# Attention times a gated token mixer on one core: where the last two heads' second span is divided, and where two output blocks are computed

## Chip, core and metric

The kernel runs on one core of a Trainium2 chip (trn2). The metric is device time in microseconds (us); the kernel before was timed at 1625.78 us, the median of three runs. The core's engines are named as the profile names them: PE (TensorE matmuls; PEld is its weight load), DVE (VectorE), ACT (ScalarE), POOL (GpSimd) and SP (SyncE, which here issues nearly all DMAs). SBUF is the on-chip memory that all of them reach, PSUM the accumulator that PE writes; PSUM has eight banks in this kernel, four called `sc`, three `mx`, one `av`.

## What is computed

```python
x  = A_x                                   # (1, 2048, 512), fp32
xn = layernorm(x)
# attention: 32 heads of 16
q, k, v = split(xn @ wqkv)                 # per head
o = softmax(q @ k.T / 4) @ v               # per head, 2048 x 2048 scores
s = concat(o) @ wo
# token mixer: an MLP along the token axis, 2048 -> 1792 -> 2048
h = layernorm(xn)
g = silu((gelu(h.T @ w1 + b1) @ w2 + b2).T)
out = x + s * g
```

## The kernel before

Everything is fp32 outside. A matmul that needs the accuracy is made of three products of a value's upper part (`[:, 0]`, fp32r) and its lower part (`[:, 1]`, the rest after subtraction): upper x upper, upper x lower, lower x upper.

**The main loop.** Heads are handled in 16 pairs, queries in two spans of 1024, keys in blocks of 128. The loop over `s` (L1274 on) takes two key blocks a turn; a turn is called a pair in this text. In every pair PE makes eight score matmuls for the row maxima (`mx`, L532, reduced by DVE at L536), eight score matmuls 22 steps behind (`sc`, L999, exponentiated by ACT at L1004 into `prob`), two groups of values (`av`, L1015), and some products of a queue called `fill`, written D in the order strings. `ORDERS` and `BEGIN` say in which order these matmuls stand in a pair, for 0, 4, 5 or 6 D; `BEGIN` holds only an entry for a first pair with six. Matmuls of 48 to 64 rows run two at a time, on the upper and the lower half of PE's rows, so one D costs one such slot.

**The fill.** It holds first the token mixer (14 blocks of 48 products, then 16 blocks of 42), then the output. `count()` (L1167 on) spreads each mixer block over as many pairs as give 16/3 products a pair; the block whose number is `SLOW` gets more pairs. 48 products so take nine pairs (6, 6, 6 and six times 5), 42 take eight. When the mixer is done, `both_pairs` runs two pairs at a time around one output block of nine products.

**The output.** Token block b (128 tokens, 16 of them) is the sum over four groups of eight heads of `oc[g, b // 4]` (attention result, heads x 16 = 128 rows, upper and lower part, 512 tokens) by the rows of `wo` of that group. Blocks 0 to 13 (`PARTS` = 14) get groups 0 to 2 in the main loop, nine products each; `part` (L919) evicts the sum with ACT (L922), POOL multiplies by the gate `g_d[b]` and adds x (L925, L926), SP stores it as `y_d[b]`. Group 3 can't be finished there: its heads 30 and 31 are the last pair.

**The ending** is `s` from `NU` = 512 on: no maxima are left, only scores, values and D, at three D a pair (`a_half`, the first of two halves) and from `s` = 524 six. In it come the group 3 products of blocks 8 to 13 and then 0 to 7, three each (42 in all). `finish` (L975) multiplies the sum with the gate and adds it to `y_d`, both on DVE, and writes out blocks 0 to 7. For blocks 8 to 15, which are the second span, rows 96 to 127 of `oc[3, 2]` and `oc[3, 3]` (heads 30 and 31) are zero (`made`, L790).

**After the last pair** (L1368 on) the second span of heads 30 and 31 is in PSUM as `av`: numerators and denominators of both heads and both halves of the span, 32 rows each. ACT copies it (`ev`). `one` turns it with four transposes so that tokens are rows, takes the reciprocal of the denominators, and spreads it over 32 columns a piece (L843, L845); `two` turns the spread reciprocals back (L854); `times` and `lower` multiply `ev` in its old layout and split it (L858, L859, L94). As that layout isn't the one of `wo`, `load_last_w` loads the rows of `wo` for the two heads once more into two zeroed tiles, and `split_last_w` splits them (L897). Each of blocks 8 to 15 then gets three products of these (`product`, L101 to L103). Blocks 14 and 15 get all four groups here as well, 24 products, `beside` (L1375), which are also used to keep PE busy during the division. `gated` (L1406) multiplies a block by its gate, `added` (L1410) adds what was summed before, on POOL or DVE, `in_parts` does both in two halves for the last block (L1417, L1418), and SP writes the blocks out (L1411, L1419).

Of the kernel before, what the change touches and what calls it, by code (L numbers as in the profile page):

```python
# [21 lines left out]
def tile_attention_token_mixer(ctx, tc, x, wqkv, wo, w1, b1, w2, b2, out):  # L22
# [746 lines left out]
    def divide(m, g, span):  # L769
# [17 lines left out]
        if last:  # L787
            for c in range(2):
                made.append(hu.tile([P, 2, 512], F32R, name="hu"))
                nc.gpsimd.memset(made[c][DH * n :, :, :].bitcast(F32), 0.0)  # L790
# [40 lines left out]
    def own(span, ev):  # L831
        rq = sm.tile([P, 4, 4], F32, name="rq", bufs=1)
        wide = el.tile([P, 512], F32, name="t", bufs=4)

        def one(pl=ps_mx, nm="mx", spread=1):

            ps = pl.tile([P, 512], F32, name=nm)
# [6 lines left out]
            for k in range(0, 4, 4 // spread):  # L844
                nc.vector.tensor_copy(  # L845
                    wide.rearrange("p (k j r) -> p k j r", k=4, j=4)[:, k : k + 4 // spread],
                    rq[:, k : k + 4 // spread].unsqueeze(3).to_broadcast([P, 4 // spread, 4, 32]),
                )

        def two(pl=ps_mx, nm="mx", ks=range(4)):  # L850

            ps = pl.tile([P, 512], F32, name=nm)
            for k in ks:
                nc.tensor.transpose(ps[:, k * P : (k + 1) * P], wide[:, k * P : (k + 1) * P], ident)  # L854
            return ps

        def times(ps, of, at):
            nc.vector.tensor_tensor(out=ev[:, at], in0=ps[:, at], in1=ev[:, at], op=OP.mult)  # L858
            nc.scalar.copy(of[:, 0, at], ev[:, at])  # L859

        def lower(of, at):
            sub(nc.vector, of[:, 1, at], ev[:, at], of[:, 0, at])

        if span == QH - 1:
            asides.extend((one, two, times, lower))
            return

        def move_in():
            ps = two()
            of = el.tile([P, 2, 512], F32R, name="uo")  # L870
            times(ps, of, slice(0, 512))
            lower(of, slice(0, 512))
# [7 lines left out]


    last_w = {}

    def load_last_w():
        for c in range(2):
            raw = last_w[c] = wp.tile([P, 4, P], F32, name="raw", bufs=3).rearrange("p a b -> p (a b)")
            nc.gpsimd.memset(raw, 0.0)
            for a in range(2):
                row = 32 * (2 * a + c) + DH * a
                h = H - 2 + a  # L890
                nc.gpsimd.dma_start(raw[row : row + DH, :], wo[DH * h : DH * (h + 1), :])

    def split_last_w():
        for c in range(2):
            raw = last_w[c]
            w = last_w[c] = el.tile([P, 2, 512], F32R, name="uo")
            nc.scalar.copy(w[:, 0, :], raw)  # L897
            after(2 + 2 * c, lambda w=w, raw=raw: sub(nc.vector, w[:, 1, :], raw, w[:, 0, :]))


# [6 lines left out]
    PARTS = NB // 2 + 6  # L907
    blocks = list(range(NB // 2, PARTS)) + list(range(NB // 2))

# [39 lines left out]
    def load_out(n):  # L949
        b = blocks[n]  # L950
        y, g = (("xt", "gt"), ("u", "sq"))[n % 2]
        if b < NB // 2:
            ys[b] = el.tile([P, D], F32, name=y)
            nc.sync.dma_start(ys[b], y_d[b])
        gts[b] = el.tile([P, D], F32, name=g)
        nc.sync.dma_start(gts[b], g_d[b])
# [3 lines left out]
    def plan_halves():  # L960

        rows = [oc[g, c][:, m, :].bitcast(F32) for c in range(NC - 1) for g in range(ND - 1) for m in range(2)]
        own = PARTS - NB // 2
        for n in range(own, len(blocks) - 3):
            b = blocks[n]
            in_halves.extend(((ys, b, y_d[b]), (gts, b, g_d[b])))
# [8 lines left out]
    def finish(n, ps):  # L975
        b = blocks[n]
        half = PARTS - NB // 2 <= n < len(blocks) - 3
        r = el.tile([P, D], F32, name="t", bufs=4) if half else gts[b]
        nc.vector.tensor_tensor(out=r, in0=ps, in1=gts[b], op=OP.mult)
        o = ys[b] if b >= NB // 2 else r  # L980
        nc.vector.tensor_tensor(out=o, in0=ys[b], in1=r, op=OP.add)
        if b < NB // 2:
            nc.sync.dma_start(out[b * P : (b + 1) * P, :], r)
        if n + 3 < PARTS - NB // 2:
            load_out(n + 3)
        elif n < PARTS - NB // 2:
            load_out(n + len(blocks) - PARTS + NB // 2)
# [35 lines left out]
    def rest():  # L1023
# [20 lines left out]
        for b in range(PARTS):  # L1044
# [6 lines left out]
        yield from until(lambda: now[0] >= NU and (ND - 1, QH - 1) in divided)  # L1051
        for n in range(3):
            load_out(n)
        plan_halves()
        for n, b in enumerate(blocks):
            if b == 0:
                yield from until(lambda: own_done and (ND - 1, 0) in divided)
# [3 lines left out]
            yield lambda n=n, ps=ps: finish(n, ps), back  # L1061
# [28 lines left out]
    SLOW = 4  # L1090
# [76 lines left out]
    def count():  # L1167
# [10 lines left out]
        return min(6, -(-left // -(-3 * left // (15 if i == SLOW else 16)))) if left > 0 else 0  # L1178
# [95 lines left out]
    for s in range(0, total + 1, 2):  # L1274
# [53 lines left out]
        else:  # L1328


            for i in range(2):

                a_half(*(heads[a][1][2 * i : 2 * i + 2] for a in range(2)), i == 0 or s >= NU + 2 * (PARTS - NB // 2))
# [8 lines left out]
            if s == NU + 4:  # L1342
                load_last_w()
            for _ in in_halves[:2]:
                load_half()
            if s == total - 6:
                split_last_w()
# [75 lines left out]
    for k in range(5):  # L1423
        if k < 4:
            times(shares[k], of, cols[k])
# [46 lines left out]
```

## Time and profile before

| | |
|---|---|
| three runs | 1625.33, 1625.78, 1626.55 us |
| profiled execution, span from first to last instruction | 1622.0 us |
| median less span (what lies around it) | 3.8 us |
| mean granted PE clock | 0.999 of full speed |
| PE, DVE, ACT, POOL busy | 1615.0, 1423.3, 1195.1, 561.6 us |
| last values matmul ends | 1604.4 us |
| last matmul ends | 1617.3 us |
| last output DMA is issued | 1619.0 us |

No separate time is given for the profiled execution; its span is the number against which a change is summed here. A busy share is an average over stages: the phase up to 150 us is projections, then comes the main loop to about 1550 us, the ending from there to 1604 us, and 18 us after the last values matmul. A busy PE is not PE at its peak, as its ends are modelled.

### The profile page before, as it was taken

The numbers are of one execution on the slowest core, as the hardware profiler recorded it, in microseconds if no ns is written. First come the engines' busy times: TensorE is split into PE (matmuls) and PEld (weight loads), VectorE is DVE, ScalarE is ACT, GpSimd is POOL, SyncE is SP. The second block draws the span as 40 slices with busy tenths as digits, with TensorE's granted clock in tenths as the row PEclk, the third lists the DMA queues.
The fourth block names the chain that finished last, engine by engine and source line by source line (L and its number), as shares of the span: only waits on it lengthen the run. The fifth ranks groups of instructions, "written<-read, shape, count | busy, mean of one in ns | idle before, by whom it ended". The sixth has DMA issues, their size and how long they took to land.

```text
span 1622.0 us, 31241 instructions
## 1 busy us (share of the span) xinstructions
PE 1615.0 (100%) x11937; PEld 877.2 (54%) x11937; DVE 1423.3 (88%) x2493; ACT 1195.1 (74%) x2311; POOL 561.6 (35%) x661
## 2 busy tenths in 40 slices
PE   9999999999999999999999999999999999999998
PEld 7888854544555544554554554545544544454544
DVE  7665999999999999999999999999999999999966
ACT  3333477777777777777877787777777778888885
POOL 1224844342244332342333332322222333642430
PEclk9999999999999999999999999999999999999999
DMA  7478441515133141826151522305151515444355
GB/s 237 181 242 204 114 92 41 95 41 75 41 70 73 30 82 34 241 70 108 41 86 38 82 65 40 77 22 76 38 85 37 112 39 84 123 101 130 106 192 192
DMA packets 152402, 155.60 MB, mean 96 GB/s; under 512 B 51564, under 2 KB 110188, under 8 KB 149180
## 3 DMA queue, kind: packets, MB, share of 16 engines
q1 hardware_dynamic: 147964, 152.87, 38.9%
q8 instruction: 94, 1.54, 0.4%
q0 software_dynamic: 4288, 0.73, 0.3%
q14 instruction: 56, 0.46, 0.1%
HBM read 101.86 MB, written 50.58 MB: 94 GB/s over the span
## 4 chain that ended last, share of the span: by engine, by line
PE 98%; DVE 1%; ACT 1%; DMA 0%; SPq 0%; issue 0%; POOL 0%; DVEq 0%
PE av L1015 31%; PE dn L1156 25%; PE sc L999 16%; PE mx L532 13%; PE sc L435 3%; PE dn L671 3%; PE mx L435 2%; PE av L435 1%; PE sc L101 0%; PE sc L103 0%; PE sc L102 0%; ACT prob L1004 0%; DVE mxp L536 0%; PE mx L999 0%; PE dn L1200 0%; PE mx L103 0%
## 5 line engine op out<-in xcount | busy, mean ns | idle before, releaser
L536 DVE TENSOR_REDUCE mxp<-mx 128x1 f32<-128x512 f32 x2026 | 1250.1, 680 | 116.1 <-PE mx L532 85.0
L1004 ACT ACTIVATE prob<-sc 128x512 f32<-128x512 f32 x2004 | 1040.4, 606 | 282.3 <-PE sc L999 117.6
L532 PE MATMUL mx<-big 48*128 48x512 f32 x2026 | 771.1, 418 | 0.1
L999 PE MATMUL sc<-big 50*128 50x512 f32 x2004 | 734.5, 411 | 0.0
L1015 PE MATMUL av<-prob,vp 128*32 128x512 f32 x4096 | 545.6, 604 | 0.3 <-DVE ev L722 0.2
L1156 PE MATMUL dn<-hu,wh 64*128 64x512 f32 x1520 | 508.0, 404 | 0.0
L999 PEld LDWEIGHTS sc<-big 50*128 50x128 f32 x2004 | 355.6, 186 | 230.0 <-ACT prob L1004 205.2
L532 PEld LDWEIGHTS mx<-big 48*128 48x128 f32 x2026 | 356.9, 185 | 187.7 <-DVE mxp L536 168.7
L1156 PEld LDWEIGHTS dn<-hu,wh 64*128 64x128 f32 x1520 | 271.8, 184 | 74.3 <-issue 49.5
L1156 PE MATMUL dn<-hu,wl 64*128 64x512 f32 x762 | 302.4, 397 | 0.0
L1015 PEld LDWEIGHTS av<-prob,vp 128*32 128x32 f32 x4096 | 80.9, 108 | 177.3 <-issue 165.0
L94 POOL TENSOR_TENSOR wl<-raw,wh 128x512 fp32r<-128x512 f32 x124 | 150.9, 1219 | 60.5 <-ACT wh L166 26.9
L1156 PEld LDWEIGHTS dn<-hu,wl 64*128 64x128 f32 x762 | 140.5, 184 | 12.6
L164 POOL CAST wh<-raw 128x512 fp32r<-128x512 f32 x104 | 60.6, 583 | 196.0 <-PE mx L532 76.0
L560 POOL CAST m<-f 16x128 fp32r<-16x128 f32 x31 | 8.7, 280 | 304.0 <-DVE f L548 303.9
L98 POOL DMA_DIRECT2D big<-m x124 | 65.8, 537 | 0.0
L1156 PE MATMUL dn<-wh,hu 64*128 64x512 f32 x168 | 59.7, 408 | 0.0
L621 POOL TENSOR_TENSOR sq<-u 128x512 f32<-128x512 f32 x11 | 11.5, 1041 | 133.8 <-ACT u L615 133.7
L708 POOL TENSOR_SCALAR t<-t 128x512 f32<-128x512 f32 x16 | 23.8, 1489 | 83.4 <-ACT t L705 83.4
L435 PE MATMUL sc<-xt,big 128*128 128x512 f32 x184 | 44.3, 389 | 0.0
L94 POOL TENSOR_TENSOR hu<-hx,hu 128x512 fp32r<-128x512 f32 x16 | 20.4, 1294 | 67.7 <-ACT hu L278 67.7
L671 PE MATMUL dn<-hu,wh 64*128 64x512 f32 x128 | 42.3, 392 | 0.0
(235 smaller groups left out, 1214.9 us busy)
## 6 DMA issues: line engine op xcount, KB each, us to landing
raw<-in_B_w_dram SPq DMA_DIRECT2D x104, 256.0 KB
big<-k_d SPq DMA_DIRECT2D x96, 128.0 KB
big<-q_d SPq DMA_DIRECT2D x96, 128.0 KB
q_d<-sg SPq DMA_DIRECT2D x16, 512.0 KB
k_d<-sg SPq DMA_DIRECT2D x16, 512.0 KB
num_d<-ev SPq DMA_DIRECT2D x30, 256.0 KB
u_d<-uo SPq DMA_DIRECT2D x14, 512.0 KB
hu<-u_d SPq DMA_DIRECT2D x14, 512.0 KB
```

The lines of the kernel that those rows point to most:

```text
L94: eng.tensor_tensor(out=o, in0=a, in1=b.bitcast(F32), op=OP.subtract)
L98: queue.dma_start(dst.bitcast(F32), src.bitcast(F32))
L164: nc.gpsimd.tensor_copy(whs[n][:, :m, :], raws[n][:, :m, :])
L435: nc.tensor.matmul(ps, w[part][:, kd, m], xt[kd][:, z, :], start=w is wh and z == 0 and kd == 0, stop=w is wl and kd == ND - 1,)
L532: nc.tensor.matmul(ps, q[o : o + 48, r * P : (r + 1) * P], k[o : o + 48, c * 512 : (c + 1) * 512], start=True, stop=True,)
L536: nc.vector.tensor_reduce(mxp[u // 16][:, a, r % 8, c : c + 1], ps, axis=AX.X, op=OP.max)
L671: nc.tensor.matmul(ps, w(slice(0, 64)), m(slice(0, 64)), start=first, stop=last)
L708: nc.gpsimd.tensor_scalar(t, t, 1.0, None, op0=OP.add)
L999: nc.tensor.matmul(ps, ks[p][o : o + 50, kb * P : (kb + 1) * P], qs[p][o : o + 50, at : at + 512], start=True, stop=True,)
L1004: nc.scalar.activation(e, ps, AF.Exp, scale=scale)
L1015: nc.tensor.matmul(av[32 * j : 32 * j + 32, :], vps[p][:, kb, 16 * a : 16 * a + 32], prob.pop((t, a, c)), start=kb == 0, stop=kb == NB - 1,)
L1156: made.append(lambda r=r, start=first and a == lead, stop=last and a != lead: nc.tensor.matmul(ps, w(r), m(r), start=start, stop=stop,))
```

## The change

The second span of heads 30 and 31 is now divided while tokens are rows. After the first four transposes and the two reciprocals, four DVE multiplications read the turned numerators in PSUM and write the quotients into a zeroed tile (`apart`, cleared by POOL at `s` = 528) at the columns that are rows 96 to 127 of the group. Eight transposes turn this back, two for each half of each of the two chunks; ACT copies rows 96 to 127 as the upper part straight into `oc[3, 2]` and `oc[3, 3]`, DVE subtracts for the lower part. So these operand tiles become complete, and blocks 8 to 15 get group 3 once, after the last pair, with the ordinary weights (24 products). The zeroing of rows 96 to 127, `load_last_w`, `split_last_w` and the group 3 products of blocks 8 to 13 in the ending are gone.

The places that these left in the ending are filled: `PARTS` is 15, of which the main loop does 13 and the ending's first pairs do blocks 13 and 14, group by group in turns, so that two PSUM banks are held at once. Only block 15 is summed after the last pair (nine products in place of 24). As the main loop has one output block less, `SLOW` names two more mixer blocks, 8 and 11, which take ten pairs (eight with 5, two with 4) in place of nine. The last additions are shared out anew: blocks 0 to 4 of the closing order on POOL, then the split block, then two on DVE.

```diff
-    PARTS = NB // 2 + 6
+    PARTS = NB - 1
+    LATE = NB - 3
+    HALVES = 5
...
-        for b in range(PARTS):
+        def whole_part(b):
             yield from until(lambda: all((g, b // (NB // QH)) in divided for g in range(ND - 1)))
...
+        for b in range(LATE):
+            yield from whole_part(b)
+        yield from until(lambda: now[0] >= NU)
         plan_halves()
-        for n, b in enumerate(blocks):
...
+        late = [whole_part(b) for b in range(LATE, PARTS)]
+        for n in range(ND - 1):
+            for turn in late:
+                yield from (itertools.islice(turn, 3) if n < ND - 2 else turn)
+        yield from until(lambda: own_done and (ND - 1, 0) in divided)
+        for b in range(NB // 2):
...
-    SLOW = 4
+    SLOW = (4, 8, 11)
...
-        return min(6, -(-left // -(-3 * left // (15 if i == SLOW else 16)))) if left > 0 else 0
+        return min(6, -(-left // -(-3 * left // (15 if i in SLOW else 16)))) if left > 0 else 0
...
-    one, two, times, lower = asides
+    ev, = asides
...
+    turned = ps_sc.tile([P, 512], F32, name="sc")
+    for k in range(4):
+        nc.tensor.transpose(turned[:, cols[k]], ev[:, cols[k]], ident)
+    some(3)
...
+            nc.vector.tensor_tensor(
+                out=spread[:, c, :, 96 + DH * a : 112 + DH * a], in0=turned[:, :, j, DH * a : DH * a + DH],
+                in1=rq[:, :, j].unsqueeze(2).to_broadcast([P, 4, DH]), op=OP.mult,
+            )
...
+            for k in (2 * h, 2 * h + 1):
+                nc.tensor.transpose(back[c, h][:, cols[k]], spread[:, c, k, :], ident)
+            if c == 0:
+                some(1)
...
+            nc.scalar.copy(o[96:, 0, at], back[c, h][96:, at])
+            sub(nc.vector, o[96:, 1, at], back[c, h][96:, at], o[96:, 0, at])
...
-        w = last_w[n % 2]
-        three(sums[b], of[:, 0, at], of[:, 1, at], w[:, 0, :], w[:, 1, :], new, True)
+        o, at = oc[ND - 1, b // 4], cols[n // 2]
+        three(sums[b], o[:, 0, at], o[:, 1, at], *wide, new, True)
...
-    for first, apart, last in ((0, 0, 2), (3, 3, 5), (6, None, 6)):
...
+    for n in range(8):
         product(n)
+    for n in range(7):
+        gated(n)
+        if n < 5:
+            added(n, nc.gpsimd)
+    in_parts(7)
+    for n in (5, 6):
+        added(n, nc.vector)
```

How the instructions move. First PE in the main loop, where mixer block 8 (`dn_5277`) begins behind block 7 (`dn_4532`); `mx` and `sc` are scores, `av` values. Before:

```order
L1156 MATMUL dn_4532<-hu_165,wl_4618 128x512
L1015 MATMUL av_5145<-prob_5226,vp_3798 32x512
L1015 MATMUL av_5145<-prob_5240,vp_3798 32x512
L1015 MATMUL av_5145<-prob_5200,vp_3798 32x512
L1015 MATMUL av_5145<-prob_5209,vp_3798 32x512
L1156 MATMUL dn_5277<-hu_150,wh_4862 128x512
L532 MATMUL mx_5289<-big_1372,big_1371 128x512
L1156 MATMUL dn_5277<-hu_150,wh_4862 128x512
```

And now:

```order
L1123 MATMUL dn_4532<-hu_165,wl_4618 128x512
L1123 MATMUL dn_5277<-hu_150,wh_4862 128x512
L962 MATMUL sc_5285<-big_1371,big_1372 128x512
L1123 MATMUL dn_5277<-hu_150,wh_4862 128x512
L533 MATMUL mx_5290<-big_1372,big_1371 128x512
L1123 MATMUL dn_5277<-hu_150,wl_4863 128x512
L962 MATMUL sc_5294<-big_1371,big_1372 128x512
L1123 MATMUL dn_5277<-hu_151,wh_4862 128x512
```

The first pair of that block has five products where it had six, and takes the ordinary order of five, in which the values stand inside the pair and not at its start.

Then PE after the last pair: `sc<-ident` are transposes, `dn_23339` and `dn_23285` the block that is summed beside (`beside`). Before, from the first four transposes on:

```order
L840 MATMUL sc_23345<-ident_136,ev_23335 128x128 x4
L1375 MATMUL dn_23339<-wl_20151,hu_20515 128x512
L1375 MATMUL dn_23339<-wh_20150,hu_20515 128x512
L1375 MATMUL dn_23339<-wh_20154,hu_20925 128x512
L854 MATMUL sc_23359<-ident_136,t_23338 128x128
L854 MATMUL sc_23361<-ident_136,t_23338 128x128
L854 MATMUL sc_23363<-ident_136,t_23338 128x128
L854 MATMUL sc_23365<-ident_136,t_23338 128x128
L1375 MATMUL dn_23339<-wl_20155,hu_20925 128x512
L101 MATMUL sc_23380<-uo_23212,big_1482 128x512
```

And now:

```order
L1358 MATMUL sc_23291<-ident_136,ev_23283 128x128 x4
L1341 MATMUL dn_23285<-wl_20284,hu_20645 128x512
L1341 MATMUL dn_23285<-wh_20283,hu_20645 128x512
L1341 MATMUL dn_23285<-wh_20287,hu_21073 128x512
L1375 MATMUL sc_23305<-ident_136,uo_23161 128x128 x2
L1341 MATMUL dn_23285<-wl_20288,hu_21073 128x512
L1375 MATMUL sc_23309<-ident_136,uo_23161 128x128 x2
L1375 MATMUL sc_23312<-ident_136,uo_23161 128x128 x2
L1341 MATMUL dn_23285<-wh_20287,hu_21073 128x512
L1375 MATMUL sc_23316<-ident_136,uo_23161 128x128 x2
L102 MATMUL sc_23327<-wh_20470,hu_22388 128x512
```

The second set of transposes is eight in place of four, with two products among them, and the first product of a block follows behind the last of them.

Last, SP at its end, where the output blocks are written. Before:

```order
L983 DMA out_dram<-sq 128x512
L983 DMA out_dram<-gt 128x512
L983 DMA out_dram<-sq 128x512
L1411 DMA out_dram<-prob 128x512 x7
L1419 DMA out_dram<-prob 128x256 x2
```

And now:

```order
L948 DMA out_dram<-t 128x512
L948 DMA out_dram<-gt 128x512
L948 DMA out_dram<-sq 128x512 x2
L1402 DMA out_dram<-prob 128x512 x5
L1410 DMA out_dram<-prob 128x256 x2
L1402 DMA out_dram<-prob 128x512 x2
```

The five blocks that POOL adds go out first, the two halves of the split block behind them, and two whole blocks last, where the two halves were last.

More of the change, by code (lines that the diff above doesn't have):

```diff
@@ L1 @@
+import itertools
 from contextlib import ExitStack
@@ L879, in own, with clear_apart @@
         after(1, lambda: asides.extend((one, move_in)))
[L882 to L898, printed above, removed]
+    apart = []
+    def clear_apart():
+        apart.append(el.tile([P, 2, 512], F32, name="uo"))
+        nc.gpsimd.memset(apart[0], 0.0)
     xts = {}
@@ L962, in plan_halves @@
         rows = [oc[g, c][:, m, :].bitcast(F32) for c in range(NC - 1) for g in range(ND - 1) for m in range(2)]
-        own = PARTS - NB // 2
-        for n in range(own, len(blocks) - 3):
-            b = blocks[n]
+        for b in range(HALVES):
             in_halves.extend(((ys, b, y_d[b]), (gts, b, g_d[b])))
```

127 lines of the change are left out of this document (47 added, 80 removed).

## Prediction

> **What bounds the kernel now.** I read the page first: engines, then the chain of work that ended last.
>
> ```profile
> PE 1615.0 (100%) x11937; PEld 877.2 (54%) x11937; DVE 1423.3 (88%) x2493; ACT 1195.1 (74%) x2311; POOL 561.6 (35%) x661
> PE 98%; DVE 1%; ACT 1%; DMA 0%; SPq 0%; issue 0%; POOL 0%; DVEq 0%
> ```
>
> PE leads nearly everywhere, so matmul slots that vanish should show as time. But the change works in three stages, and each has its own second in line. The windows by stage give it (columns: stretch, its length, busy us of PE, PEld, DVE, ACT, POOL, granted clock, DMA share, GB/s).
>
> ```profile
> 500.00:600.00 100.00, 100.00 (x774) 50.93 (x772) 92.21 (x160) 77.57 (x152) 38.80 (x49) 1.00 0.29 59
> 1400.00:1500.00 100.00, 99.89 (x760) 49.83 (x760) 93.64 (x160) 85.28 (x169) 44.54 (x43) 1.00 0.47 120
> 1560.00:1580.00 20.00, 19.83 (x148) 7.67 (x146) 8.56 (x15) 19.07 (x39) 2.57 (x5) 1.00 0.69 227
> 1580.00:1600.00 20.00, 20.00 (x150) 8.76 (x150) 10.96 (x16) 18.75 (x38) 0.00 (x0) 1.00 0.77 267
> 1600.00:1622.00 22.00, 17.11 (x87) 11.13 (x79) 14.83 (x35) 4.67 (x11) 2.60 (x2) 0.95 0.33 120
> ```
>
> In the main loop DVE is at 92%, late in it at 94%, so it is close behind PE. In the ending's first pairs ACT is at 95%; DVE and POOL have room. After 1604 PE is no longer alone: the chain there goes through DVE and ACT, then 40 products, then DVE, then the last transfer.
>
> ```profile
> 1602.12 2.32 PE av L1015 x16
> 1604.44 1.13 PE dn L1375 x4
> 1605.57 0.45 PE sc L840 x4
> ...
> 1606.17 0.17 DVE rq L843
> ...
> 1606.36 0.63 DVE t L845 x4
> ...
> 1607.08 0.30 DVE ev L858
> ...
> 1607.40 0.31 ACT big L859
> ...
> 1607.75 0.50 PE sc L101
> ...
> 1617.02 0.24 PE dn L103
> ...
> 1617.28 0.43 DVE prob L1417
> ...
> 1618.53 0.42 DVE prob L1418
> ```
>
> From 1607.75 to 1617.26 PE runs one product after another (some 0.23 each). DVE ends at 1618.95, the span at 1622.0: 3.1 us are the last store and the program's end.
>
> **The main loop: one output block less, two mixer blocks with a pair more.** Each block is evicted by one ACT instruction, so the distance between these is the time of a block.
>
> ```profile
> L615 ACT ACTIVATE u<-dn,b1t x9: 692/692/693, 296.2 to 695.2; 128x512 f32<-128x512 f32 x9
> L704 ACT ACTIVATE ev<-dn,b2h x16: 692/692/701, 739.4 to 1402.4; 128x512 f32<-128x512 f32 x16
> L922 ACT COPY t<-dn x14: 627/629/654, 1412.1 to 1551.9; 128x512 f32<-128x512 f32 x14
> ```
>
> A nine-pair block (three pairs of six products, six of five) takes (695.2 - 296.2)/8 = 49.88 us; an eight-pair block (two of six, six of five) (1402.4 - 739.4)/15 = 44.20; an output block in two pairs with nine products (1551.9 - 1412.1)/13 = 10.75. So a pair of six is 49.88 - 44.20 = 5.68, a pair of five (44.20 - 2 x 5.68)/6 = 5.47, and a product about 0.21. A pair of four is then 5.26. The new block of eight fives and two fours takes 8 x 5.47 + 2 x 5.26 = 54.28, which is 4.40 more than nine pairs. Twice 4.40 less 10.75 gives -1.95 us. The count of slots says the same: nine products go at the 0.23 of a product in the ending (rows below), -2.1. I take **-1.9**. Bounds: if a pair of four is held at the pace of five by DVE, the block takes 54.7, and it is 9.64 - 10.75 = -1.1; the other end is -2.1 with nothing lost where the block begins. That both blocks now begin in the ordinary order of five, with the values inside the pair, has no row: nothing, or a slot of 0.23 each, which the bound of -1.1 covers.
>
> DVE's work in a mixer pair is 92% of 5.47, 5.03, so a pair of four at 5.26 isn't yet waiting for it.
>
> **The ending's pairs.** The same 42 products stand in the same pairs, so PE's work is unchanged. A pair of three products is 4.02 us, and the half with the products is 2.36 against 1.66: 0.23 a product.
>
> ```profile
> 1560.97 1.06 PE L1015 MATMUL av<-prob,vp 128*32 128x512 f32 x8
> 1563.33 1.07 PE L1015 MATMUL av<-prob,vp 128*32 128x512 f32 x8
> 1564.99 1.06 PE L1015 MATMUL av<-prob,vp 128*32 128x512 f32 x8
> 1563.78 1.14 ACT L1004 ACTIVATE prob<-mx 128x512 f32<-128x512 f32 x2
> 1594.15 0.87 SPq L973 DMA_DIRECT2D hu<-g_d  x2
> ```
>
> What goes is off the path: twelve DVE operations of `finish`, POOL's memsets and its loads of `wo`, ACT's two splits; DVE and POOL are below 60% here, and ACT did the splits in the six-product pairs where it has slack. Cost of removing them: nothing gained. What comes: two ACT copies of 0.63 (L922), and POOL's four operations, hidden. The first copy falls in a three-product pair, where ACT has 4.02 x 0.05 = 0.2 to spare. It is late by 0.4, and PE's next scores want free banks: two of the seven now belong to `dn`. The exponentials of one half end at 1564.92, while the next half's scores are due when the values begun at 1563.33 are through, 0.5 before that; the fourth of them then waits for a bank. I take **+0.2**, between 0 (the six-product pairs give it back first) and +0.6. SP issues as many DMAs as before: six gate loads go, the loads, stores and reloads of the two blocks come, at 0.43 a DMA (row above) in pairs of over 4 us. The two reloads wait for their own stores to land, with output stores queued behind them that nobody waits for; the loads for blocks 5 to 7 are issued three pairs later, and are used three pairs after that. Nothing, unless a wait of over 10 us stands in that queue.
>
> **After the last pair.** Up to the reciprocals nothing changes. The four copies (L845, 0.63 together) become four multiplications of 64 elements; I take the same time, as the nearest rows on both sides are a reciprocal of 8 elements, 0.17, and L858 of 128, 0.30. The first two are done at about 1606.72, their two transposes are read by ACT from 1607.3. Then PE does a product (0.23), four transposes (0.45 by L840), a product and two transposes: the first of the 24 final products starts at about 1608.45, and the last ends at 1608.45 + 24 x 0.232 + 0.16 = 1614.2. PE ends 3.1 us sooner than the 1617.26 of now: fifteen products less (3.5), four transposes and a longer way round more.
>
> That gain isn't handed on, since behind PE there is now a longer tail.
>
> ```profile
> 1609.20 1.28 DVE L1406 TENSOR_TENSOR prob<-sc,hu 128x512 f32<-128x512 f32 x2
> 1610.03 1.30 POOL L1410 TENSOR_TENSOR prob<-big,prob 128x512 f32<-128x512 f32 x1 [44.90 <-DVE prob L1406]
> 1610.99 0.89 DVE L1410 TENSOR_TENSOR prob<-big,prob 128x512 f32<-128x512 f32 x1
> 1611.80 0.68 DVE L1410 TENSOR_TENSOR prob<-big,prob 128x512 f32<-128x512 f32 x1
> 1613.23 1.30 POOL L1410 TENSOR_TENSOR prob<-big,prob 128x512 f32<-128x512 f32 x1 [1.90 <-DVE prob L1406]
> 1614.20 0.87 DVE L1410 TENSOR_TENSOR prob<-big,prob 128x512 f32<-128x512 f32 x1
> 1611.36 6.00 SPq L1411 DMA_DIRECT2D out_dram<-prob  x7
> 1618.19 1.12 SPq L1419 DMA_DIRECT2D out_dram<-prob  x2
> ```
>
> The fourth subtraction needs the last transposes, ACT's copy and DVE: about 1609.45. Behind it in DVE's queue stands the first gate (0.68), done at 1610.13, and 0.15 later POOL begins, as it did behind the first of the two gates at 1609.20. POOL now has five additions in a row: 5 x 1.30 + 4 x 0.05 = 6.7, ending at 1617.0. DVE's own: seven gates, four half operations of 0.42, two additions, 0.64 x 7 + 1.7 + 1.4 = 7.6 after 1609.45, or 1617.0 too.
>
> The two are not independent. A DVE addition that reads two SBUF tiles and starts during a POOL addition took 0.89 and 0.87, and 0.68 when POOL was idle; both long ones ended 0.55 after POOL's did, so they waited for it. In the new tail the two half additions meet POOL's fourth and fifth. That POOL is kept waiting by DVE no row shows (1.30 both times, but it came first); it is between nothing and 0.42 for each half addition, and I take one: POOL ends at about 1617.4.
>
> [...]
>
> SP takes its queue in order: the fifth store at 1617.4, behind it the two halves and the last two whole blocks, which have waited, at 0.43 each. The last one is issued at about 1619.1, as now (1618.19 + 1.12 less its own issue), but it holds 256 KB and not 128, and 1 MB is issued in 1.6 us. In the DMA line for 1600 to 1622.1 (slices of 0.55 us) the rate tops out at 389 GB/s, and the first stored bytes are counted about 0.8 after their issue.
>
> ```profile
> GB/s 0 0 26 408 41 0 0 319 156 0 0 0 0 0 0 0 0 30 0 0 0 0 345 382 389 300 15 59 386 378 389 219 256 219 176 93 206 0 0 0
> ```
>
> 1 MB at 385 takes 2.7: from 1618.2 to 1620.9, where now the last bytes go in the slice that ends at 1620.45. That is +0.45; with POOL never kept waiting it is +0.05. I take **+0.4**, between -1.3 (the second rival) and +0.9 (POOL kept waiting twice).
>
> **The sum** is -1.9 + 0.2 + 0.4 = -1.3 us: the span goes from 1622.0 to 1620.7, and the median, 3.8 above the span of the profiled execution, from 1625.78 to **1624.5**. A measurement of this kernel can tell 0.2%, 3.25 us, from no change; this is less.
>
> **Rivals.**
>
> Second, the tail follows PE. If POOL's chain doesn't bind (it begins sooner or its additions take turns with DVE's better than I think), the end hangs on the last product: two more additions of 0.68 on DVE and 0.35 for the larger last store behind 1614.2, in place of 1617.26. That is -3.1 + 1.4 + 0.35 = -1.3 for this stage, and with -1.9 and nothing lost in the ending's pairs -3.2, up to -3.6 with all of the slots: 1622.4. For it: DVE and POOL both come out at 1617.0, so little decides. Against it: SP's order, which puts the DVE blocks behind POOL's fifth. Chance 0.22.
>
> Third, the main loop saves less because DVE sets the pace of a pair of four: -1.1 there, the rest as summed, -0.5: 1625.3. For it is DVE's 94% in the window of the output blocks; against it that the mixer's pairs, where the fours stand, have a lower share. Chance 0.18.
>
> Fourth, slower: the banks. With two banks held through five pairs, the scores of a half have five banks. If all four of them had to wait for the exponentials of the half before, each half would lose 0.5, ten halves 5.0: 1625.78 - 1.9 + 0.4 + 5.0 = 1629.3. It decides as soon as ACT runs a good 0.3 later than now throughout, because then the fourth score's bank, five back, is not yet read when PE comes to it. Against it: ACT catches up in a pair of six, and only two copies are added. Chance 0.08.
>
> Fifth, the change doesn't change the work it names: the pairs' sizes come from `count()`, and if the two fewer pairs of output blocks were given back as idle pairs the main loop would gain nothing: 1626.4, with the other terms. The order has all 13 blocks in the main loop and no pair without products but those at its end, so 0.04.
>
> My forecast has 0.48.
>
> **How the numbers follow.** The forecast's own bounds are 1623.8 (-2.1 + 0 + 0.1) to 1626.2 (-1.1 + 0.6 + 0.9). The range takes in the second and the third rival, and of the unpriced first pair and the tail what goes beyond: 1622.0 to 1627.0; outside lie the fourth and the ends of the second. Faster by over 0.2% means below 1622.5: three fifths of the second rival and a small part of the forecast, 0.17. Slower by over 0.2%, above 1629.0, is the fourth and a little for what I haven't seen, 0.10. Within: 0.73.
>
> **What would show it.** In the profile of the changed kernel: the output copies (L922's successor) still 10.7 to 10.8 apart, and two mixer evictions 54.0 to 54.7 apart; the last values matmul 1.4 to 2.1 sooner than 1604.4, else the main loop or the banks are mis-sized; score matmuls between 1555 and 1575 that wait for ACT would speak for the fourth rival; the first final product 4.0 after the last values matmul, the last one 9.8 after; five POOL additions end to end up to some 13 after it; DVE half additions of about 1 us rather than 0.42; the stores of the DVE blocks issued right behind POOL's fifth. If the last store is issued before POOL's fifth addition ends, or more than 0.6 sooner relative to the last values matmul than now (14.5), my tail is wrong.

## The result, and the profile after

The changed kernel takes 1644.62 us (median of four runs, 1643.77 to 1645.78), the kernel before 1625.55 beside it on the same chip: a ratio of 1.0120, with a 95% interval of 1.0105 to 1.0134. It is slower by 19 us, where the forecast was 1.3 us faster and the range ended at 1627.0. The profiled execution has a span of 1643.3 us and a time of 1645.09.

The page of the changed kernel: busy times, two of the 40-slice rows, the chain by engine, and one of the costliest groups.

```profile
PE 1613.8 (98%) x11908; PEld 875.8 (53%) x11908; DVE 1413.7 (86%) x2472; ACT 1195.1 (73%) x2310; POOL 563.8 (34%) x659
PE   9999999999999999996999999999999999999996
PEclk9999999999999999998999999999999999999998
PE 98%; DMA 1%; DVE 0%; SPq 0%; issue 0%; ACT 0%; DVEq 0%; POOL 0%; POOLq 0%
L1123 PE MATMUL dn<-hu,wh 64*128 64x512 f32 x1520 | 507.2, 404 | 13.4 <-DMA hu<-u_d 13.4
```

PE's busy time fell by 1.2 us, as a change with fewer matmuls should, and its share went from 100% to 98%. There are two holes: one in the nineteenth slice (about 740 to 780 us), far from every place that the prediction weighed, and one in the last. The mixer's products waited 13.4 us, in one piece, for the DMA that brings a hidden block back (`hu<-u_d`).

The evictions by ACT give the stages. L616, L705 and L895 are the L615, L704 and L922 of before; the last group has two late blocks behind the thirteen of the main loop.

```profile
L616 ACT ACTIVATE u<-dn,b1t x9: 691/692/713, 296.2 to 704.4; 128x512 f32<-128x512 f32 x9
L705 ACT ACTIVATE ev<-dn,b2h x16: 691/692/692, 764.4 to 1427.6; 128x512 f32<-128x512 f32 x16
L895 ACT COPY t<-dn x15: 631/633/756, 1437.4 to 1596.5; 128x512 f32<-128x512 f32 x15
```

Against the rows of before: the last hidden block (the fourteenth of the mixer) is evicted at 704.4 and not 695.2, +9.3 for the two long blocks (9.64 was the bound). From there to the first output block of the mixer it is 60.0 us where it was 44.2: **+15.8**. The other fifteen take 663.2 (663.0). From the last of them to the last copy of the main loop (1566.5 in the trace) it is 138.9 in place of 149.5: -10.6. From that copy to the start of the last values (1602.9 before, 1618.3 now) it is 51.8 in place of 51.0, +0.8; and from there to the end, a stretch called the tail below, 25.0 in place of 19.1, **+5.9**. The sum is +21.4; the spans differ by 21.3. (The times differ by 19, as the profiled execution of before was a short one. In the executions for which both are known, time is 1.7 to 2.4 above span, mostly 1.8, so its own time must have been near 1624, not the median of 1625.78; the "3.8" above the span in the prediction mixed two executions.)

**The hole at 744 us.** SP's timeline of before, around the return of the last hidden block (`u_d<-uo` is its store, `hu<-u_d` its reload, `d<-ev` and `num_d<-ev` store the finished span of a pair of heads, and `big<-k_d` is the first of the twelve loads for the next pair):

```profile
710.50 0.34 SPq L98 DMA_DIRECT2D u_d<-uo  x1
...
714.18 0.34 SPq L98 DMA_DIRECT2D hu<-u_d  x1
...
738.37 1.09 SPq L734 DMA_DIRECT2D d<-ev  x2
...
740.00 0.37 SPq L98 DMA_DIRECT2D big<-k_d  x1
```

And of the changed kernel, with SP's longest wait in it (us in total, times, longest) and PE's timeline behind it:

```profile
719.75 0.34 SPq L99 DMA_DIRECT2D u_d<-uo  x1
...
736.82 1.08 SPq L735 DMA_DIRECT2D d<-ev  x2
737.95 0.40 SPq L739 DMA_DIRECT2D num_d<-ev  x1
738.44 0.37 SPq L99 DMA_DIRECT2D big<-k_d  x1
...
746.02 0.30 SPq L99 DMA_DIRECT2D big<-q_d  x1
747.06 0.38 SPq L133 DMA_DIRECT2D vp<-v_d  x1
748.16 5.19 SPq L99 DMA_DIRECT2D hu<-u_d  x1
```

```profile
SPq L735 <- ACT ev L725: 16.2, 1, 16.2
```

```profile
743.03 0.40 PE L533 MATMUL mx<-big 48*128 48x512 f32 x1
756.85 0.79 PE L1123 MATMUL dn<-hu,wh 64*128 64x512 f32 x1 [13.42 <-DMA hu<-u_d]
```

Before, the reload is issued 3.7 us behind its store, 24 us ahead of the transfers at the end of the head pair. Now it stands behind them: three stores of the pair's result, the twelve loads and the load of `vp`. The first of these stores waits 16.2 us for ACT's copy of the result, the last thing that the head pair makes. In both timelines SP issues one DMA after another in the order of the program, and these transfers take it another 11.3 us (736.82 to 748.16). So it comes to the reload 28 us behind the store. It lands 8.6 us later, and PE's next product needs it.

The windows around it (columns as before) show what the idle time cost beyond itself: the granted clock, 1.00 from 700 to 744, averages 0.64 in the hole and is at a half for some 4.5 us of full work behind it.

```profile
744.00:757.00 13.00, 0.15 (x2) 0.15 (x2) 0.54 (x1) 0.00 (x0) 0.55 (x1) 0.64 1.07 157
757.00:761.00 4.00, 4.00 (x18) 1.49 (x20) 0.69 (x1) 1.19 (x2) 0.00 (x0) 0.50 0.78 220
761.00:765.00 4.00, 4.00 (x32) 1.40 (x28) 3.71 (x6) 3.16 (x6) 0.00 (x0) 0.96 0.71 156
```

13.4 of waiting and about 2.3 at half speed make the 15.8. From PE's return at 756.85 it took some 4.5 us to the full clock: 0.50 from 757 to 761, and 0.96 from 761 to 765 is a half until 761.3. Half of 4.5 is the 2.3.

**The hole at the end.** POOL, DVE and SP behind the last products, the DMA line (slices of 0.68 us from 1616.0 on), and POOL's closing instructions, the drains that stand at the end of its program (count, shortest/median/longest in ns, first and last start):

```profile
1625.56 6.42 POOL L1401 TENSOR_TENSOR prob<-big,prob 128x512 f32<-128x512 f32 x5 [24.68 <-DVE prob L1397]
```

```profile
1629.78 1.09 DVE L1409 TENSOR_TENSOR prob<-big,prob 128x256 f32<-128x256 f32 x1
...
1631.23 1.03 DVE L1409 TENSOR_TENSOR prob<-big,prob 128x256 f32<-128x256 f32 x1
```

```profile
1632.43 0.88 SPq L1410 DMA_DIRECT2D out_dram<-prob  x2
1633.41 0.90 SPq L1402 DMA_DIRECT2D out_dram<-prob  x2
```

```profile
GB/s 135 78 105 372 393 414 399 192 9 0 0 0 0 0 24 0 0 315 72 369 72 324 138 246 117 360 342 381 336 0 0 0 0 0 0 0 0 0 0 0
L1445 POOLq DRAIN  x3: 40/106/14447, 1628.1 to 1643.0; - x3
```

The last bytes go at 1635.8, 17.5 behind the start of the last values, where it was 17.4 before: up to here the tail costs +0.1. But then nothing moves for 7.5 us. POOL's additions end at 1625.56 + 6.42 = 1631.98, and its closing drain, taken up at 1628.1, lasts 14.45 us, until 1642.53, 10.55 behind the last addition. The last drains of the other engines start only then, at 1642.8, and the program ends. Before, the same row read

```profile
L1468 POOLq DRAIN  x3: 46/102/2312, 1613.2 to 1621.8; - x3
```

and that drain was over at 1615.5, 0.98 behind its last addition and long before SP was done. No row of the chain of waits names it: the chain ends with DVE's last addition.

**The ending's pairs.** PE, ACT and PE again:

```profile
1568.41 0.50 PE L962 MATMUL sc<-big 50*128 50x512 f32 x1 [0.18 <-ACT prob L967]
```

```profile
1592.22 0.64 ACT L895 COPY t<-dn 128x512 f32<-128x512 f32 x1
1592.68 1.16 ACT L967 ACTIVATE prob<-mx 128x512 f32<-128x512 f32 x2
```

```profile
1593.56 1.39 PE L978 MATMUL av<-prob,vp 128*32 128x512 f32 x8
```

In the first pair a score waits for an exponential to free its bank and the next values come 0.47 later than before; at 1593.56 values take 1.39 in place of 1.07, as their exponentials stand behind the copy of a late block, 0.31 more. That is the +0.8.

### The profile page after: what moved, and what is told of

Same layout as the page of the kernel before. It is cut to its first block, busy times and chain, and to the rows that moved or that the text cites. A ratio compares the mean times of both kernels' runs of the same rounds, so it can differ in the third digit from the quotient of the medians.

```text
span 1643.3 us, 31131 instructions
## 1 busy us (share of the span) xinstructions
PE 1613.8 (98%) x11908; PEld 875.8 (53%) x11908; DVE 1413.7 (86%) x2472; ACT 1195.1 (73%) x2310; POOL 563.8 (34%) x659
## 4 chain that ended last, share of the span: by engine, by line
PE 98%; DMA 1%; DVE 0%; SPq 0%; issue 0%; ACT 0%; DVEq 0%; POOL 0%; POOLq 0%
PE av L978 31%; PE dn L1123 24%; PE sc L962 16%; PE mx L533 14%; PE dn L672 3%; PE sc L436 3%; PE mx L436 2%; PE av L436 1%; DMA hu<-u_d 1%; PE sc L102 0%; PE sc L104 0%; PE sc L103 0%; DMA big<-q_d 0%; PE dn L1167 0%; PE mx L340 0%; PE mx L102 0%
## 5 line engine op out<-in xcount | busy, mean ns | idle before, releaser
L1123 PE MATMUL dn<-hu,wh 64*128 64x512 f32 x1520 | 507.2, 404 | 13.4 <-DMA hu<-u_d 13.4
L1123 PE MATMUL dn<-wh,hu 64*128 64x512 f32 x156 | 55.3, 407 | 0.0
```

Of the source, the lines that this page charges most:

```text
L1123: made.append(lambda r=r, start=first and a == lead, stop=last and a != lead: nc.tensor.matmul(ps, w(r), m(r), start=start, stop=stop,))
```

## Experiments

The first question was whether the place of the reload in SP's queue makes the hole, and whether the drain belongs to the additions. The kernel before was run beside them, for its span and its drain.

> The kernel before, unchanged, for its span beside its time in the same execution. In the changed kernel time less span is 1.8 us in all executions, and its span ends 7.4 us after the last byte of output, since POOL's closing drain lasts until then. If what lies around the span is 1.8 here too, this profile's span is about 1623.8; if it is 3.8, 1622. If the long drain belongs to the five additions, POOL's drain here ends about 1 us after its last addition, as in the first profile of before; if it comes in some executions whatever POOL did, this profile can show one that is 5 us or longer.

Measured: 1624.59 beside 1624.26 for before (ratio 1.000, 0.9991 to 1.0010), a span of 1623.2 for a time of 1624.95, and a drain that ends 0.99 behind the last addition. What lies around the span is 1.8. Its last values start 1.1 later than in the first profile, with nothing changed: sums of profiled spans are good to about 1 us here.

```diff
-                if i == NF and kb == NF - 3:
+                if i == NF and kb == NF - 5:
```

> The changed kernel, with the reload of the last hidden block asked for two blocks of rows (six products, about one pair) sooner, so that it stands ahead of the head pair's twelve loads in SP's queue. Theory of the queue: the reload is issued about 3 us after its own store, PE's idle time of 13.4 us at the mixer's products is gone, the first silu eviction comes 44.2 to 44.5 after the last gelu one (59.9 now), and the time falls by 15 to 16 us, to about 1629. Rival, the hidden block itself is late because blocks 8 and 11 took a pair more: the store is issued at the same time as now and the products still wait, so 1640 or more stays.

Measured: 1628.77 (ratio to before 1.0027, 1.0016 to 1.0038). SP's timeline and the evictions:

```profile
719.32 0.34 SPq L99 DMA_DIRECT2D u_d<-uo  x1
...
722.37 0.34 SPq L99 DMA_DIRECT2D hu<-u_d  x1
...
737.98 0.37 SPq L99 DMA_DIRECT2D big<-k_d  x1
```

```profile
L616 ACT ACTIVATE u<-dn,b1t x9: 692/692/713, 295.9 to 704.0; 128x512 f32<-128x512 f32 x9
L705 ACT ACTIVATE ev<-dn,b2h x16: 688/692/693, 748.2 to 1411.3; 128x512 f32<-128x512 f32 x16
```

The store comes when it did; the reload follows 3 us later, and the first output block 44.2 behind the last hidden one, 15.8 less than in the changed kernel. Against the kernel before, timed beside each, the loss falls from 19.1 to 4.5 us. One DMA is asked for six products sooner, and nothing else is different. The rival falls: the last hidden block comes as late as in the changed kernel, and nothing waits for it.

```diff
-    SLOW = (4, 8, 11)
+    SLOW = (4, 16, 20)
```

> The changed kernel with the two long blocks behind the hand-over from hidden to output blocks (blocks 16 and 20, nine pairs in place of eight) and not ahead of it. Theory of the queue: nothing shifts against the head pairs until the reload is done, so the wait is gone and the time is 1628 to 1630, with two evictions 48.4 to 49 apart. If the price is in the ten-pair blocks and not in the place, PE still loses some 15 us somewhere and the time stays above 1640.

Measured: 1629.90 (1.0034, 1.0022 to 1.0046); reload 3.8 us behind its store, two evictions 49.0 and 49.1 apart, the others 44.0 to 44.3. So two longer blocks make no hole where they stand behind the reload; it was the place.

```diff
     for n in range(7):
         gated(n)
-        if n < 5:
+        if n in (0, 3):
             added(n, nc.gpsimd)
+        if n in (2, 5):
+            added(n - 1, nc.vector)
+            added(n, nc.vector)
+    added(6, nc.vector)
     in_parts(7)
-    for n in (5, 6):
-        added(n, nc.vector)
```

> The changed kernel with the last additions shared out as before: blocks 0 and 3 of the closing order on POOL, five on DVE, the split block last. Theory of the drain: POOL's closing drain ends about 1 us after its last addition, the span ends 1.5 us after the last byte; DVE needs 9.5 us from its first gate, which is 0.7 later than now, so the end comes about 6 us sooner: span 1637, time 1638 to 1639. Rival, the drain isn't tied to the additions: it is as long again and the time is 1645.

Measured: 1642.80 (1.0113, 1.0098 to 1.0128), and the theory was wrong. DVE ends 0.6 later after the last values than in the changed kernel, as expected, but the drain still ends 10.55 behind POOL's last addition, as in the changed kernel; the tail falls from 25.0 to 23.0 only because this addition ends 2.0 sooner. The number of additions doesn't set the drain. What the four kernels with the long drain have in common against before is something that I had counted as free: POOL's four loads of `wo` in the ending are gone, and its clearing of a tile has come. The next four take this apart.

```diff
+    def load_aside():
+        raw = wp.tile([P, 4, P], F32, name="raw", bufs=3).rearrange("p a b -> p (a b)")
+        for n in range(4):
+            nc.gpsimd.dma_start(raw[32 * n : 32 * n + DH, :], wo[DH * n : DH * (n + 1), :])
...
+            if s == NU + 4:
+                load_aside()
```

> The kernel of reload_early with four DMAs issued by POOL at s = 516, as before issued its four loads of wo (here rows that nobody reads). POOL's closing drain ended 10.55 us after POOL's last addition in four kernels that issue no DMA from POOL in the ending, and 0.98 us after it in both profiles of before, which does. Theory of the missing DMAs: the drain ends about 1 us after the last addition, the span ends 1.5 us after the last byte, the tail falls from 25.0 to about 19.1, and the time from 1628.8 to 1623. Rival, the clearing of the tile by POOL or something else in the new tail: the drain stays at 10.5 and the time at 1628.8.

Measured: 1622.99, beside 1624.39 for before (0.9990, 0.9981 to 1.0000). The drain ends 0.99 behind the last addition, the tail is 18.9. Four DMAs that nobody reads win 5.8 us.

```diff
-        nc.gpsimd.memset(apart[0], 0.0)
+        nc.vector.memset(apart[0], 0.0)
```

> The kernel of reload_early with the tile cleared by DVE in place of POOL. Theory of the missing DMAs: POOL's drain still ends 10.5 us after its last addition, the tail stays at 25.0. Rival, the clearing: about 1 us and a tail of 19.1.

Measured in one execution: 1628.87, drain 10.55, tail 24.9. The clearing has no part in it.

```diff
-        if n < 5:
-            added(n, nc.gpsimd)
+        added(n, nc.vector)
     in_parts(7)
-    for n in (5, 6):
-        added(n, nc.vector)
```

> The kernel of reload_early with all last additions on DVE, the split block last. POOL is then free after its clearing, some 20 us before the last values matmul, and a drain of 10.5 us is over long before SP's; DVE needs 7 x 0.68 us for gates and as much for additions and 1.7 for the halves, 11 from its first gate: its end comes 17.3 after the last values matmul (15.1 now), the span ends 3.1 later, a tail of 20.4 in place of 25.0, and the time is about 1624.2. If the late end isn't POOL's drain but another thing of the new tail, the tail grows by 2.

Measured: 1624.29 (1.0000, 0.9990 to 1.0009); the tail is 20.1. The drain is still long (12.8 us), but it runs from 1581.9 to 1594.7, beside the last pairs, and nobody waits for it. It ends 10.55 behind POOL's last work here too, which is the clearing. That the late end is POOL's drain is shown from a second side.

```diff
-                nc.gpsimd.dma_start(raw[row : row + DH, :], wo[DH * h : DH * (h + 1), :])
+                nc.sync.dma_start(raw[row : row + DH, :], wo[DH * h : DH * (h + 1), :])
```

> The kernel before, with the four loads of wo in the ending issued by SP and not by POOL; nothing else. Theory of the missing DMAs: POOL's drain now ends 10.5 us after its last addition (at 14.5 + 10.5 = 1625 in the times of the first profile), 3.8 behind SP's closing waits, and the time rises by 3.8 us, to 1628. Rival, something in the new tail: the drain stays at 1 us and the time at 1624.3.

Measured: 1628.00 (1.0021, 1.0012 to 1.0031). One word changed in the kernel before, and it is 3.6 us slower: its drain ends 10.55 behind the last addition.

```profile
L1468 POOLq DRAIN  x3: 40/102/11876, 1613.7 to 1626.1; - x3
```

Is it how long ago POOL issued its last DMA, or how many?

```diff
-        for n in range(4):
+        for n in range(1):
```

> The kernel of early_pool_dma with one DMA from POOL at s = 516 in place of four. If it is enough that POOL issued any DMA in the ending, its closing drain ends about 1 us after its last addition and the tail is 18.9, as with four. If the number counts, the drain is longer, up to 10.5 us, and the tail up to 25.0.

Measured in one execution: 1623.68, drain 0.75 behind the last addition, tail 18.9. One is enough.

```diff
-            if s == NU + 4:
-                load_aside()
...
+        if s == 470:
+            load_aside()
```

> The kernel of early_pool_dma with the same four DMAs from POOL at s = 470, ahead of POOL's last regular DMA (at about 1525, 90 us ahead of the end) and not behind it. If what counts is how long ago POOL's last DMA was, the drain is long again (10.5 us behind the last addition, tail 25.0, time 1628.8). If it is the number of POOL's DMAs in the whole program (134 and not 130, as before), the drain takes 1 us and the time is 1623.

Measured in one execution: 1623.90, drain 0.99, tail 18.9. So it isn't how long ago, but the number or the kind. (The number that was expected here is off by two: the traces count 132 and 128 DMAs from POOL, not 134 and 130.)

```diff
-            nc.gpsimd.dma_start(ks[p][row : row + 2, :].bitcast(F32), ones)
+            nc.sync.dma_start(ks[p][row : row + 2, :].bitcast(F32), ones)
```

> The kernel of reload_early with the four small DMAs that POOL issues at the start (rows of ones) issued by SP: POOL issues 124 DMAs in all and none of the kind that reads wo. The kernels with a long closing drain (10.55 us behind the last addition) issue exactly 128 from POOL; those with a short one (0.98) 129 or 132. Theory of the count: 124 isn't 128, so the drain takes 1 us, the tail is 18.9 and the time 1623, though POOL has fewer DMAs than ever. Theory of the kind (a DMA from the chip's main memory must be among POOL's): the drain stays at 10.55, the time at 1628.8.

Measured: 1629.05 (1.0028, 1.0018 to 1.0038). The theory of the count, as I had put it (128 and no other number), is wrong: with 124 the drain is long, yet a little shorter, 10.21.

```profile
1609.15 6.43 POOL L1401 TENSOR_TENSOR prob<-big,prob 128x512 f32<-128x512 f32 x5 [24.66 <-DVE prob L1397]
```

```profile
L1445 POOLq DRAIN  x3: 46/98/14093, 1611.7 to 1626.3; - x3
```

```diff
-        for n in range(4):
-            nc.gpsimd.dma_start(raw[32 * n : 32 * n + DH, :], wo[DH * n : DH * (n + 1), :])
+        nc.gpsimd.memset(raw[:8, :], 0.0)
+        nc.gpsimd.dma_start(raw[8:9, :], raw[:1, :])
```

> The kernel of reload_early with one more DMA from POOL at s = 516, from SBUF to SBUF like its regular ones (129 in all), behind a small memset. Theory of the count: drain 1 us, tail 18.9, time 1623. Theory of the kind: 10.55, 25.0, 1628.8.

Measured in one execution: 1623.08, drain 0.75, tail 18.9. Kind and size made no difference here: with one more DMA within SBUF, of 2 KB, the drain is the same 0.75 as with one of 32 KB from main memory.

```diff
-        for n in range(4):
-            nc.gpsimd.dma_start(raw[32 * n : 32 * n + DH, :], wo[DH * n : DH * (n + 1), :])
+        for n in range(16):
+            nc.gpsimd.dma_start(raw[8 * n : 8 * n + 8, :], wo[DH * n : DH * n + 8, :])
```

> The kernel of early_pool_dma with sixteen small DMAs from POOL at s = 516 in place of four, 144 in all. If the drain is long whenever the count is a multiple of 16, it takes 10.55 us behind the last addition and the tail is 25.0; if 128 is the step (or 32 or 64), or if the kind decides, about 1 us and 18.9.

Measured in one execution: 1622.72, tail 18.9, but the drain is longer again, 1.97, and hidden behind SP's end:

```profile
1609.26 6.43 POOL L1408 TENSOR_TENSOR prob<-big,prob 128x512 f32<-128x512 f32 x5 [24.67 <-DVE prob L1404]
```

```profile
L1452 POOLq DRAIN  x3: 46/102/5843, 1611.8 to 1620.7; - x3
```

Put side by side, the drain follows the number of DMAs that the program issued from POOL, as the traces count them:

| DMAs from POOL | drain ends behind POOL's last addition | kernels |
|---|---|---|
| 124 | 10.21 us | ones_on_sp |
| 128 | 10.55 us | the changed kernel, five of its variants, before_sp_loads |
| 129 | 0.75 us | one_pool_dma, sbuf_pool_dma |
| 132 | 0.98 to 0.99 us | before, before_again, early_pool_dma, far_pool_dma, dve_copies, four_on_pool |
| 144 | 1.97 us | pool_144 |

From 129 to 144 it is (1.97 - 0.75)/15 = 0.08 us for each DMA; from 124 to 128, 0.085; and if 132 is taken as 4, (10.21 - 0.99)/120 = 0.077 from there to 124. One line of 0.67 and 0.08 a DMA meets all five within 0.4 us, if the count begins anew past 128. Why it should do so no run shows. (One of the five variants at 128 is early_dve_only, which has no addition on POOL; there it is 10.55 behind the end of the clearing.)

Last, two versions of the whole. First the late blocks' copies on DVE:

```diff
-        nc.scalar.copy(y, ps)
+        (nc.vector.tensor_copy if now[0] >= NU else nc.scalar.copy)(y, ps)
```

> The kernel of early_pool_dma with the two late output blocks copied out of their banks by DVE and not by ACT. The ending's pairs took 60.97 us against 60.2 before; 0.31 of it is a pair whose values wait for exponentials behind such a copy. If the copies on ACT are that cost, the pairs take 60.65 and the time falls by 0.3, to 1622.7; if DVE's own copies delay the division of heads there, nothing is gained. Against before: 0.998 to 1.0.

Measured: 1623.44, beside 1624.89 for before (0.9990, 0.9981 to 0.9999). From the last copy of the main loop to the start of the last values it is 51.5 us, where early_pool_dma has 51.8, so the 0.3 is where it was said to be; the time alone couldn't tell it from early_pool_dma. It is the version whose interval lies, just, below before.

```diff
-        if n < 5:
+        if n < 4:
             added(n, nc.gpsimd)
+        else:
+            added(n, nc.vector)
     in_parts(7)
-    for n in (5, 6):
-        added(n, nc.vector)
```

> The kernel of dve_copies with four of the last additions on POOL and three on DVE, and the split block last. In it DVE's two half additions took 1.09 and 1.03 beside POOL's last additions, 0.42 alone: 1.3 is won, 0.7 for one more addition on DVE is lost, and the last store is half as large (0.35). DVE's end comes about 0.6 sooner, the span 0.9: tail 18.0 in place of 18.9 and the time 1622.5 where before has 1624.9 (0.9985). If DVE's whole additions wait for POOL's as the halves did, nothing is won.

Measured: 1623.35, beside 1624.58 (0.9992, 0.9983 to 1.0001); the tail is 19.1, nothing won. DVE and POOL in its timeline:

```profile
1613.57 1.05 DVE L1408 TENSOR_TENSOR prob<-big,prob 128x512 f32<-128x512 f32 x1
...
1615.26 1.04 DVE L1408 TENSOR_TENSOR prob<-big,prob 128x512 f32<-128x512 f32 x1
```

```profile
1609.80 5.94 POOL L1408 TENSOR_TENSOR prob<-big,prob 128x512 f32<-128x512 f32 x4 [25.32 <-DVE prob L1404]
```

Four additions on POOL take 5.94 where five took 6.42: its third and fourth are 1.77 and 1.71 long in the trace, where alone they are 1.30, while DVE's take 1.05 and 1.04 in place of 0.68. Beside each other both are longer, and the exchange won nothing on either side.

## Why the prediction was wrong, step by step

**The main loop, where it failed.** The step reads: "Twice 4.40 less 10.75 gives -1.95 us. The count of slots says the same." As a price of matmuls it was good. In the changed kernel the long blocks and the missing output block come to +9.3 + 0.2 - 10.6 = -1.1, which is its bound; with the hole closed (early_pool_dma) the ending begins 1.3 to 2.5 us sooner than in the two profiles of before. What failed is that only products were counted. A mixer block that is moved by two pairs carries its DMAs with it. From block 12 on, everything in the mixer stands two pairs later against the head pairs, whose boundaries didn't move, and at such a boundary SP issues stores that wait for the head pair's result and thirteen loads behind them. The prediction walked through SP's queue in the ending, where it found nothing ("Nothing, unless a wait of over 10 us stands in that queue"), and not where the change moves 21 mixer blocks (9 to 29). A wait of just that kind stood in it: 16.2 us in SP's queue, of which PE lost 13.4, and 2.3 of half clock behind that.

**"Cost of removing them: nothing gained."** This was said of POOL's loads of `wo`, among others. Removing them cost 5.8 us, since POOL's closing drain went from 0.98 to 10.55 us and became the last thing to end. No row that the prediction read shows the drain; the view of the program's last line does, with 2.3 us, and SP's end hid it.

**The tail up to the last byte** was mis-sized by little: +0.1 against +0.4. The first final product starts 3.95 behind the last values (4.0 was said), the last ends 9.4 behind them (9.8), the two half additions on DVE take 1.09 and 1.03 ("about 1 us"), and the stores of DVE's blocks are issued right behind the others. The rate of the DMA line doesn't top out at 389, as the prediction says: its own row has 408, and that of the changed kernel 414. That DVE's half additions keep POOL waiting was put in once, at 0.42; no run shows that term. POOL's fifth addition took 1.45 in place of 1.30, 0.15 more, so 0.42 was too much in this tail. But POOL's additions can be longer beside DVE's by as much: four_on_pool has the rows, 1.77 and 1.71.

**The ending's pairs** cost +0.8 where +0.2 was said and +0.6 was the bound. The mechanism was the right one, a score that waits for a bank (0.47) and exponentials behind a copy (0.31), each in a pair of its own.

**The rivals.** Neither the forecast nor one of its four rivals is what happened. The third's condition is near what the traces show: the two long blocks take 54.70 and 54.85 us, where 54.28 was forecast and 54.7 is a pair of four held at the pace of five; that DVE holds it isn't shown. The fourth, slower by waiting scores, is there with 0.47 of its 5.0. The second, a tail that follows PE, and the fifth, pairs given back idle, are excluded by the rows above. A third kind was missing: a wait far from the edited lines, in a queue whose order the edit turns.

With both causes taken away (early_pool_dma) 1622.99 to 1624.39 is -1.40 us, where -1.3 was forecast. That it is so close is in part luck. The main loop's term was about right (-1.9, against the 1.3 to 2.5 us sooner above), but the ending's pairs cost 0.6 more than was said, and the tail 0.6 less: 18.9 where before has 19.1, as the end follows the last byte 1.4 us later in place of 1.7. These two cancel. What decided were the two terms that weren't there.

## What to carry to other kernels

When a change shifts a stream of work against another that has its own beat, follow the queue of the engine that issues the DMAs past the beat: which DMA was ahead of a blocked group of transfers and is now behind it. Here SP issued them in the order of the program, which is known before anything runs. And look at what ends the program, not only at what ends the work: here POOL's closing drain ended 0.98 us behind its last addition with the four loads of `wo`, and 10.55 without them, though these were issued some 50 us before.

## What the runs showed of the hardware

In these runs POOL's closing drain ended 10.21 us behind POOL's last work with 124 DMAs issued from POOL in the whole program, 10.55 with 128, 0.75 with 129, 0.98 to 0.99 with 132 and 1.97 with 144. These five counts fit an estimate of 0.67 us and 0.08 for each DMA, as if counted from the start up to 128 and from 0 again past it. The time runs from the end of POOL's last work: the changed kernel, which uses POOL nearly up to its end, paid for it with a tail of 25.0 us, and early_dve_only, whose POOL is done some 37 us ahead of the end, did not (the drain was over at 1594.7, the tail was 20.1). That the count begins anew at 128 is read from five counts; whether it does so at 256, and whether the 129th DMA pays elsewhere for what the drain no longer does, stays open. The issue of that DMA took 0.57 us in before, about as long as any other (0.50 to 0.61 for the 124 small ones of the head pairs).
